# Second products of a two-level seven-product scheme: sums carried in PSUM by ScalarE, parts in another order

## The chip, the cores and the metric

The kernel runs on one core of a Trainium2 chip. The metric is device time in microseconds (us). The profile is of one execution; the engines are named as in it: PE (matmuls), PEld (PE's weight loads), DVE, ACT (ScalarE), POOL and SP.

## The reference

The reference is an attention layer whose mask keeps only keys in the query's hash bucket, and after it an MLP mixer of two stages. Only the last stage matters here. With `x` the attention's output, in the layout (4, 768, 512):

```python
xt = x.transpose(0, 2, 1)
h = np.maximum(xt @ w_tok1, 0.0) @ w_tok2
u = x + h.transpose(0, 2, 1)
h2 = np.maximum(u @ w_ch1, 0.0) @ w_ch2
return (u + h2).astype(np.float32)
```

All of it is in fp32; `w_ch1` is 512 x 1536 and `w_ch2` 1536 x 512. The change lies in the multiplication by `w_ch2`, called the second products below.

## The kernel before

The program has three stretches: attention (to about 310 us of the profile), the token mixer (to about 387 us) and the channel mixer (function `channels`, the rest). The channel mixer works in three steps, s = 0, 1, 2, each on 1024 of the 3072 positions (two halves of 512). A step first computes the hidden rows, R = relu(w_ch1' u), and then the second products (`outputs(s)`).

Both multiplications use Winograd's form of the seven-product scheme, twice over. On the outer level the second product of a step is made of seven products p1 to p7, in the order p1, p5, p7, p6, p3, p2, p4 (`ORDER`). p1 is multiplied out plainly (`whole_product`). Each of the other six goes through `product`, which applies the seven-product scheme again: the left factor (weights) and the right factor are cut into quarters, and seven sums of left quarters are multiplied with seven sums of right quarters. With a00 to a11 the left and b00 to b11 the right quarters, and S1 = a10 + a11, S2 = S1 - a00, S4 = a01 - S2, T1 = b01 - b00, T2 = b11 - T1:

| part | left (its number in `LEFTS`) | right |
|---|---|---|
| m1 | a00 (4) | b00 |
| m2 | a01 (5) | b10 |
| m5 | S1 (0) | T1, in the place of b01 |
| m7 | a00 - a10 (1) | b11 - b01, in `extra()` |
| m6 | S2 (2) | T2 |
| m3 | S4 (3) | b11 |
| m4 | a11 (6) | b10 - T2, in the place of b10 |

With U = m1 + m6 the four blocks of the output are: block 0 = m1 + m2, block 1 = U + m5 + m3, block 2 = U + m7 + m4, block 3 = U + m7 + m5. `qs[:, 0]` to `qs[:, 3]` are these blocks, 128 x 256 each.

A part is three matmuls of 128 x 128 by 128 x 256 (a quarter is three chunks of 128 deep), and an fp32 matmul appears in the profile as two instructions. So a product has 42 matmul instructions. All matmuls are issued by `accumulate` (L780) and all of these ACT copies by `copy` (L786).

PSUM is handed out in pairs of banks, b0 to b3, in a ring: `blocks(2)` takes two pairs, one product uses two and the next the other two. `ps[0]`, `ps[1]` are the two banks of the first pair, `ps[2]`, `ps[3]` of the second.

The order of the work is written by hand (a manual schedule): each engine executes its instructions in the order of the program, and semaphores are derived from what each instruction reads and writes. In a product of before:

1. PE: m1 into ps[0], m2 into ps[1]. ACT copies m1 out (p1). DVE makes T2 in the place of b00 (L1330).
2. PE: m5 into ps[2], m7 into ps[3]. DVE makes b10 - T2 (L1334). ACT copies both m5 and m7 out in one instruction of 128 x 512 (p57).
3. PE: m6 added on ps[0], which makes U; m3 added on ps[2]; m4 added on ps[3]. ACT copies U out.
4. DVE: the work of the list `between` (sums of the outer level, L1292 and L1377, and others), then `begin` for the next product (L1287: `extra()`, L1288: T1), then four additions that finish the blocks (L1352, L1355, L1368, L1369).

`begin(name)` thus prepares the next product's right factor while this one runs. `combine` (L1292) makes the outer level's right sums, four operations of 128 x 768: for p5 it remakes r0, for p7 it remakes r1. `fetch_left` has SP fetch the left factors of the product after the next in two pieces, [0] for the first four of `LEFTS` and [1] for the last three.

`look()` is a side task on ACT: it checks the sizes of q and k to see whether the fast attention was safe. A look is a Square (L1462), a Relu that accumulates, and a read of the accumulator (L1470), all on 128 x 768, followed by a POOL issue that fetches the next piece. It does something on ACT only when three pieces have been fetched ahead. Looks stand after the copy of p1's result (L1395; s + 1 of them, none in the last step) and in each product (one in step 0, two in step 1, none in step 2). `copies()` hands out scratch tiles of 128 x 1024 from three buffers.

In the last step the products p2 and p4 are `final`: their sums are added to the output's values in place and stored from SBUF, p2 by SP, p4's last two blocks by ACT. In p4 of the other steps `inputs` (L606 to L610) prepares the next step's right factors.

Of the kernel before, what the change touches and what calls it, by code (L numbers as in the profile page):

```python
# [48 lines left out]
def kernel(  # L49
# [14 lines left out]
    P = 128  # L64
# [687 lines left out]
    def channels(pool, psum, SW1, second, TA, judge):  # L752
# [32 lines left out]
        def copy(ps, c):  # L785
            nc.scalar.copy(c, ps)  # L786
            return c
# [378 lines left out]

        ORDER = ["p1", "p5", "p7", "p6", "p3", "p2", "p4"]
        WHOLE = ["p1"]
        LEFTS = [4, 5, 0, 1, 2, 3, 6]
        halves = [slice(0, QC), slice(QC, HC)]  # L1170
        passed = second["passed"]

        def prepare():
# [12 lines left out]

                return job

            def parts(w, store, other=False):
                def job():  # L1190
                    (a00, a01), (a10, a11) = weight_quarters(w)
                    n = 4 * QC * P
                    if other:
                        place = area(1)[:, 7 * QC * P : 7 * QC * P + n].rearrange("p (i n) -> p i n", i=4)
                    else:
                        place = pool.tile([P, 2, S], F32, name="seen", tag="seen", bufs=1)
                        place = place.rearrange("p i s -> p (i s)")[:, :n].rearrange("p (i n) -> p i n", i=4)
                    new = [place[:, i].rearrange("p (k c) -> p k c", k=a00.shape[1]) for i in range(4)]
                    nc.vector.tensor_tensor(new[1], a00, a10, op=ALU.subtract)
                    nc.vector.tensor_tensor(new[0], a10, a11, op=ALU.add)  # L1200
                    nc.vector.tensor_tensor(new[2], new[0], a00, op=ALU.subtract)
                    nc.vector.tensor_tensor(new[3], a01, new[2], op=ALU.subtract)
                    store(place, [a00, a01, a11], a10)

                return job

            def second_parts(name):
                def store(place, raw, rest):
                    to = passed[name].rearrange("p (i n) -> p i n", i=7)
                    nc.sync.dma_start(out=to[:, 2:6], in_=place)  # L1210
                    for i, a in zip((0, 1, 6), raw):
                        nc.sync.dma_start(out=to[:, i].rearrange("p (k c) -> p k c", k=QC), in_=a)

                return parts(left[name], store, name == "p2")

            def hidden_parts(name):
                def store(place, raw, rest):
# [52 lines left out]
                    nc.sync.dma_start(out=left_at(g)[:, sl], in_=passed[name][:, sl])  # L1270


        operand = {f"r{i}": [[R[i][:, n, ks] for n in range(2)] for ks in halves] for i in range(4)}
        operand["x"] = [
            [t.rearrange("p a k n -> p (a k n)")[:, n * QC * TT // 2 : (n + 1) * QC * TT // 2].rearrange(
# [8 lines left out]
        def begin(name):  # L1284

            b00, b01, b10, b11 = quarters(name)
            nc.vector.tensor_tensor(extra(), b11, b01, op=ALU.subtract)  # L1287
            nc.vector.tensor_tensor(b01, b01, b00, op=ALU.subtract)  # L1288

        def combine(to, a, op, b, where=[(0, 0), (0, 1), (1, 0), (1, 1)]):  # L1290
            for h, n in where:
# [16 lines left out]
            fetch_left(7 * s + 2)  # L1308
            return pair

        def product(s, j, name, q, between, final=None):

            half = slice(0, TT // 2)
            pairs = blocks(2)
            ps = [a[:, i, half] for a in pairs for i in range(2)]
            w = left_at(7 * s + j).rearrange("p (i k c) -> p i k c", i=7, k=QC)
            b00, b01, b10, b11 = quarters(name)  # L1320
            ks = range(QC)

            def part(i, left, right, start=True):
                accumulate(ps[i], lambda k: w[:, LEFTS.index(left), k], lambda k: right[:, k], ks, start)

            part(0, 4, b00)
            part(1, 5, b10)
            c = copies()
            p1 = copy(ps[0], c[:, half])
            nc.vector.tensor_tensor(b00, b11, b01, op=ALU.subtract)  # L1330
            part(2, 0, b01)
            part(3, 1, extra())
            fetch_left(7 * s + j + 2, [0])
            nc.vector.tensor_tensor(b10, b10, b00, op=ALU.subtract)  # L1334
            p57 = copy(pairs[1][:, :, half], c[:, TT // 2 : TT * 3 // 2].rearrange("p (i t) -> p i t", i=2))
            part(0, 2, b00, False)
            part(2, 3, b11, False)
            u = copy(ps[0], c[:, TT * 3 // 2 :])
            for _ in range(min(s + 1, 2) if s < last else 0):
                look()  # L1340
            part(3, 6, b10, False)
            fetch_left(7 * s + j + 2, [1])
            for work in between:
                work()
            qs = q.rearrange("p i (n t) -> p (i n) t", n=2)

            issuer = nc.scalar if j == 6 else nc.sync
            if j < 6 and not final:
                begin(ORDER[j + 1])
            if final:  # L1350
                nc.vector.tensor_tensor(p1, p1, qs[:, 0], op=ALU.add)
            nc.vector.tensor_tensor(qs[:, 0], ps[1], p1, op=ALU.add)  # L1352
            if final:
                nc.sync.dma_start(out=final(0, 0), in_=qs[:, 0])
            nc.vector.tensor_tensor(p57[:, 0], p57[:, 0], p57[:, 1], op=ALU.add)  # L1355
            if j < 6 and final:
                begin(ORDER[j + 1])
            if final:
                nc.vector.tensor_tensor(qs[:, 3], qs[:, 3], u, op=ALU.add)
                nc.vector.tensor_tensor(qs[:, 3], qs[:, 3], p57[:, 0], op=ALU.add)  # L1360
                nc.sync.dma_start(out=final(1, 1), in_=qs[:, 3])
                for i in (1, 2):
                    nc.vector.tensor_tensor(qs[:, i], qs[:, i], u, op=ALU.add)
                for i, a in [(1, ps[2]), (2, ps[3])]:
                    nc.vector.tensor_tensor(qs[:, i], a, qs[:, i], op=ALU.add)  # L1365
                    issuer.dma_start(out=final(i // 2, i % 2), in_=qs[:, i])
                return
            nc.vector.tensor_tensor(qs[:, 3], p57[:, 0], u, op=ALU.add)  # L1368
            nc.vector.tensor_tensor(  # L1369
                qs[:, 1:3], pairs[1][:, :, half], u[:, None, :].to_broadcast([P, 2, TT // 2]), op=ALU.add,  # L1370
            )

        def outputs(s):
            sl = [slice(TT * (2 * s + i), TT * (2 * s + i) + TT) for i in range(2)]
# [21 lines left out]
            for _ in range(s + 1 if s < last else 0):  # L1396
                look()
            q7, q57, q6, q5 = [output_at(i) for i in range(4)]
            product(s, 1, "p5", q5, [lambda: combine("r0", "x", ALU.subtract, "r0")])
            rest = decide() if judge and s == last else None  # L1400
            product(s, 2, "p7", q7, [lambda: combine("r1", "r2", ALU.subtract, "x")])
            if rest:
                rest()
            product(s, 3, "p6", q6, [add(q57, q7, q5)])
            if rest:
                flags.append(nc.values_load(unsafe, min_val=0, max_val=1))
                tc.mark_branch_hint_location("careful", hint="LikelyTaken", engines=mybir.ALL_ENGINES)
# [2 lines left out]
            def add_residual():  # L1410
                nc.gpsimd.dma_start(out=q7, in_=XT[:, KC:, sl[0]], accum_op=ALU.add)

            product(s, 4, "p3", q3, [
                add(q6, q6, q1), add(q57, q57, q6), store(q57, 1, 1), add(q5, q5, q6), add(q7, q7, q6),
                *([] if s < last else [add_residual]),
            ])
            end = [add(q3, q3, q5), store(q3, 0, 1)]
            if s < last:
                product(s, 5, "p2", q2, [
                    *end, right_sums("p2", s + 1)[0],  # L1420
                    *([lambda h=h: fetch_hidden_left(h) for h in range(5)] if s == 0 else []),
                ])
                product(s, 6, "p4", q4, [
                    add(q2, q2, q1), store(q2, 0, 0), lambda: inputs(s + 1, T, 0), lambda: inputs(s + 1, T, 1),
                ])
                add(q4, q4, q7)()
                store(q4, 1, 0)()
            else:
                def final(at):
                    start = sl[0].start  # L1430
                    return lambda i, n: out[at + i, :, start + TT // 2 * n : start + TT // 2 * (n + 1)]

                product(s, 5, "p2", q1, [
                    *end, add(q1, q1, XT[:, :KC, sl[0]]),
                ], final(0))
                product(s, 6, "p4", q7, [], final(KC))

        def residual(s):

# [43 lines left out]
        def decide():  # L1483

            assert not (unseen or seen)
            top = pool.tile([P, 1], F32, name="top", tag="top", bufs=1)
            nc.vector.tensor_reduce(top, excess, AX.X, ALU.max)
            nc.vector.tensor_scalar(top, top, 1e30, None, op0=ALU.min)

            def rest():  # L1490
                ps = blocks(1)[0][:, 0]
                nc.tensor.transpose(ps[:1, :P], top, ident)  # L1492
                one = pool.tile([1, 1], F32, name="one", tag="one", bufs=1)
                nc.vector.tensor_reduce(one, ps[:1, :P], AX.X, ALU.max)
                nc.vector.tensor_scalar(unsafe, one, 0.0, None, op0=ALU.is_gt)

            return rest
# [150 lines left out]
```

## Time and profile before

| | |
|---|---|
| median of 3 runs | 792.02 us (791.40 to 792.57) |
| profiled execution | 792.34 us |
| its span | 790.5 us |
| PE busy | 782.9 us, 4721 matmul instructions |
| DVE busy | 674.3 us |
| ACT busy | 446.5 us |
| granted clock of PE | 0.999 |

The page of a profile gives busy times by engine, the chain of work that ended last, and groups of instructions. The timeline lists instructions in order of time: start, duration, engine, line, operation, output<-inputs, shapes, count, and in square brackets the idle time of the engine before it with what ended it. A matmul's duration (0.38 us here) overlaps with its successor's; the distance from start to start is 0.216 us for 256 columns.

### The profile page before, as it was taken

To read this page: it belongs to the slowest core of one execution; us is meant where nothing else is said; L and a number is where in the kernel's file an instruction comes from. 1 tells how busy PE (TensorE), PEld (TensorE's weight loads), DVE (VectorE), ACT (ScalarE), POOL (GpSimd) and SP (SyncE) were. 2 spreads that over 40 slices of the span, in tenths; PEclk is the share of its full clock that TensorE was granted. 3 is DMA by queue.
4 is the path that set the end of the run, shared out by engine and by line. 5 is a ranking of instruction groups with operands and counts; after the bars stand their busy time and mean duration, and the time that the engine had idled before them with its cause. 6 is when DMAs were issued, how large, how long until landed. Compare 5 with 4: busy or idle time off the path is not lost.

```text
span 790.5 us, 12412 instructions
## 1 busy us (share of the span) xinstructions
PE 782.9 (99%) x4721; PEld 475.6 (60%) x4721; DVE 674.3 (85%) x925; ACT 446.5 (56%) x730; POOL 53.5 (7%) x77
## 2 busy tenths in 40 slices
PE   8999999999999999999999999999999999999997
PEld 4444444444444444455544458877777887786886
DVE  5989898988887677999697879899779899978986
ACT  6688888888888887333323121326765456674111
POOL 1000000000000000011121010111001122000001
PEclk9999999999999999999999999999999999999999
DMA  4435353537352424795686995799846789820655
GB/s 164 163 123 163 123 164 123 163 123 243 137 180 89 143 66 160 203 273 123 117 268 220 344 379 174 216 305 238 259 134 210 251 230 221 266 84 0 198 167 120
DMA packets 102160, 144.85 MB, mean 183 GB/s; under 512 B 30216, under 2 KB 71888, under 8 KB 102096
## 3 DMA queue, kind: packets, MB, share of 16 engines
q1 hardware_dynamic: 93936, 119.02, 45.8%
q0 software_dynamic: 7728, 24.64, 13.8%
q8 instruction: 38, 0.62, 0.3%
q10 hardware_dynamic: 432, 0.34, 0.1%
q14 instruction: 26, 0.21, 0.1%
HBM read 101.01 MB, written 35.52 MB: 173 GB/s over the span
## 4 chain that ended last, share of the span: by engine, by line
PE 98%; DMA 1%; SPq 0%; DVE 0%; issue 0%
PE b L780 50%; PE sc L353 20%; PE acc L407 16%; PE t L653 5%; PE t L693 5%; PE sums L431 2%; PE hp L301 1%; DMA qk<-in_qk 1%; PE hw L325 0%; SPq L271 0%; DVE second L1365 0%; PE b L1492 0%; SPq L1643 0%
## 5 line engine op out<-in xcount | busy, mean ns | idle before, releaser
L360 ACT ACTIVATE e<-sc 128x768 f32<-128x768 f32 x192 | 154.2, 811 | 11.2 <-PE sc L353 10.8
L353 PE MATMUL sc<-qk 64*128 64x384 f32 x768 | 152.6, 483 | 0.0
L780 PE MATMUL b<-R,second 128*128 128x256 f32 (+1 forms) x612 | 150.9, 404 | 0.0
L780 PEld LDWEIGHTS b<-R,second 128*128 128x128 f32 x612 | 116.2, 190 | 31.7 <-issue 17.2
L407 PE MATMUL acc<-e,vn 128*32 128x384 f32 x1536 | 127.0, 486 | 0.0
L786 ACT COPY c<-b 128x512 f32<-128x512 f32 (+1 forms) x78 | 37.4, 487 | 155.0 <-PE b L780 141.2
L392 DVE TENSOR_TENSOR esd<-esd,e 128x768 f32<-128x768 f32 x96 | 92.0, 958 | 10.4 <-ACT e L360 0.5
L407 PEld LDWEIGHTS acc<-e,vn 128*32 128x32 f32 x1536 | 49.9, 110 | 73.9 <-issue 73.3
L353 PEld LDWEIGHTS sc<-qk 64*128 64x128 f32 x768 | 68.2, 187 | 41.1 <-issue 35.8
L780 PE MATMUL b<-XT,WC 128*128 128x256 f32 (+1 forms) x228 | 73.9, 469 | 0.0
L353 PE MATMUL sc<-bits 64*128 64x384 bf16 x384 | 62.5, 323 | 0.0
L780 PEld LDWEIGHTS b<-XT,WC 128*128 128x128 f32 x228 | 43.3, 190 | 25.3 <-issue 20.8
L388 DVE SCALAR_TENSOR_TENSOR esd<-e 128x768 f32<-128x768 f32 x32 | 30.6, 955 | 23.4 <-ACT e L360 23.3
L780 PE MATMUL b<-XT,SW 128*128 128x256 f32 (+1 forms) x156 | 43.7, 412 | 0.0
L653 PE MATMUL t<-x,W 128*128 128x512 f32 x96 | 41.8, 593 | 0.0
L353 PEld LDWEIGHTS <-bits 64*128 64x128 bf16 x384 | 18.5, 94 | 33.2 <-issue 10.0
L713 POOL DMA_DIRECT2D XT<-second x8 | 9.8, 1228 | 383.5 <-DVE second L712 361.2
L780 PEld LDWEIGHTS b<-XT,SW 128*128 128x128 f32 x156 | 29.6, 190 | 10.0 <-issue 5.1
L452 ACT COPY rec<-rec 32x384 f32<-32x384 f32 x64 | 32.7, 510 | 5.0 <-DVE rec L446 4.2
L413 ACT ACTIVATE num<-acc,vsum 128x384 f32<-128x384 f32 x32 | 18.6, 580 | 29.7 <-PE acc L407 29.3
L780 PE MATMUL b<-TA,WC 128*128 128x256 f32 (+1 forms) x92 | 33.6, 475 | 0.0
L395 DVE TENSOR_TENSOR esd<-esd,e 128x768 f32<-128x768 f32 x32 | 30.5, 954 | 1.9
(245 smaller groups left out, 1172.9 us busy)
## 6 DMA issues: line engine op xcount, KB each, us to landing
second<-left SPq DMA_DIRECT2D x20, 768.0 KB
raw<-in_moe_w_ch SPq DMA_DIRECT2D x16, 768.0 KB
qk<-in_qk SPq DMA_DIRECT2D x15, 768.0 KB
second<-left SPq DMA_DIRECT2D x18, 576.0 KB
seen<-in_qk POOLq DMA_DIRECT2D x21, 384.0 KB, 4.8
WC<-hidden_left SPq DMA_DIRECT2D x18, 448.0 KB
vn<-in_v SPq DMA_DIRECT2D x16, 384.0 KB
vt<-in_vT SPq DMA_DIRECT2D x16, 384.0 KB
```

The lines of the kernel that those rows point to most:

```text
L353: nc.tensor.matmul(sc[:, i, :HALF], t[rows, 1, P * c : P * c + P], t[rows, 0, qs], start=start, stop=not start,)
L360: nc.scalar.activation(e, sc[:, :, :HALF], ACT.Exp, scale=SCALE)
L388: nc.vector.scalar_tensor_tensor(self.d, es[0], NR * EPS, es[1], op0=ALU.add, op1=ALU.add,)
L392: nc.vector.tensor_tensor(self.d, self.d, e, op=ALU.add)
L395: nc.vector.tensor_tensor(self.d, self.d, self.es[-1], op=ALU.add)
L407: nc.tensor.matmul(acc[D * i + d : D * i + d + 32], vn[:, i, c, d : d + 32], e[:, i], start=(c == 0), stop=(c == NR - 1),)
L413: nc.scalar.activation(nums[self.n][:, self.half], acc, ACT.Identity, scale=-1.0, bias=vsum,)
L452: nc.scalar.copy(rec[other : other + 32, h], rec[at : at + 32, h])
L653: nc.tensor.matmul(ps, W1[:, r, P * j : P * j + P], x[:, r], start=(r == 0), stop=(r == NR - 1),)
L693: nc.tensor.matmul(ps[at], left, right, start=start, stop=True, skip_group_check=True,)
L780: nc.tensor.matmul(ps, left(k), right(k), start=start and k == ks[0], stop=stop and k == ks[-1], skip_group_check=True,)
L786: nc.scalar.copy(c, ps)
```

## The change

Two things change in `product`. First, ACT writes into PSUM: m1, once copied out, is written into b0, where m2 is added on it; U is copied from a0 to a1, where m5 and then m3 are added on it. m7 is copied out to c7 before m4 is added on it, and U + m5 to c5 before m3 is. Four additions on DVE become two (block 3 = c7 + c5, block 2 = b1 + u), and ACT copies block 0 and block 1 to their places. Second, the parts come in the order m1, m7, m6, m2, m5, m4, m3. T2 is now made in `begin` in a tile of its own (t2), and what was `between` is now `early`, ahead of b10 - T2 on DVE, or `late`, after the last part. The looks of a product are split into halves between the copies. The left factors are stored in the order in which they are used. In the final products U, c7 and c5 are added from the side, one addition follows the last part, and the stores stand at the end.

```diff
-        LEFTS = [4, 5, 0, 1, 2, 3, 6]
+        LEFTS = [4, 5, 1, 2, 0, 3, 6]
...
             nc.vector.tensor_tensor(b01, b01, b00, op=ALU.subtract)
+            t2 = copies()[:, : QC * TT // 2].rearrange("p (k n) -> p k n", k=QC)
+            nc.vector.tensor_tensor(t2, b11, b01, op=ALU.subtract)
+            begun.append(t2)
...
-        def product(s, j, name, q, between, final=None):
+        def product(s, j, name, q, early, late, final=None):
...
-            part(0, 4, b00)
-            part(1, 5, b10)
-            c = copies()
-            p1 = copy(ps[0], c[:, half])
-            nc.vector.tensor_tensor(b00, b11, b01, op=ALU.subtract)
-            part(2, 0, b01)
-            part(3, 1, extra())
+            t2 = begun.pop()
+            c1, c7, u, c5 = (a[:, i] for a in [split4(copies())] for i in range(4))
...
+            part(a0, 4, b00, True)
+            copy(a0, c1)
+            if looks > 1:
+                begin_look()
+            part(b1, 1, extra(), True)
+            copy(c1, b0)
+            copy(b1, c7)
+            if looks > 1:
+                end_look()
+            part(a0, 2, t2)
+            for work in early:
+                work()
+            if final:
+                plus(qs[:, 3], qs[:, 3], c7)
+            part(b0, 5, b10)
             fetch_left(7 * s + j + 2, [0])
-            nc.vector.tensor_tensor(b10, b10, b00, op=ALU.subtract)
-            p57 = copy(pairs[1][:, :, half], c[:, TT // 2 : TT * 3 // 2].rearrange("p (i t) -> p i t", i=2))
-            part(0, 2, b00, False)
-            part(2, 3, b11, False)
-            u = copy(ps[0], c[:, TT * 3 // 2 :])
-            for _ in range(min(s + 1, 2) if s < last else 0):
-                look()
-            part(3, 6, b10, False)
+            copy(a0, a1)
+            copy(a0, u)
+            nc.vector.tensor_tensor(b10, b10, t2, op=ALU.subtract)
+            part(a1, 0, b01)
+            if final:
+                plus(qs[:, 0], b0, qs[:, 0])
+            else:
+                copy(b0, qs[:, 0])
+            if looks:
+                begin_look()
+            part(b1, 6, b10)
+            copy(a1, c5)
+            if looks:
+                end_look()
+            part(a1, 3, b11)
             fetch_left(7 * s + j + 2, [1])
-            for work in between:
+            for work in late:
                 work()
...
-            if j < 6 and not final:
+            if j < 6:
                 begin(ORDER[j + 1])
...
-            nc.vector.tensor_tensor(qs[:, 0], ps[1], p1, op=ALU.add)
...
-            nc.vector.tensor_tensor(p57[:, 0], p57[:, 0], p57[:, 1], op=ALU.add)
...
-                for i, a in [(1, ps[2]), (2, ps[3])]:
-                    nc.vector.tensor_tensor(qs[:, i], a, qs[:, i], op=ALU.add)
-                    issuer.dma_start(out=final(i // 2, i % 2), in_=qs[:, i])
+            if not final:
+                plus(qs[:, 3], c7, c5)
+                plus(qs[:, 2], b1, u)
+                copy(a1, qs[:, 1])
                 return
-            nc.vector.tensor_tensor(qs[:, 3], p57[:, 0], u, op=ALU.add)
-            nc.vector.tensor_tensor(
-                qs[:, 1:3], pairs[1][:, :, half], u[:, None, :].to_broadcast([P, 2, TT // 2]), op=ALU.add,
-            )
+            plus(qs[:, 2], qs[:, 2], u)
+            plus(qs[:, 3], qs[:, 3], c5)
+            plus(qs[:, 2], b1, qs[:, 2])
+            plus(qs[:, 1], a1, qs[:, 1])
...
+            for i, issuer in zip((0, 3, 2, 1), (nc.sync, nc.sync, nc.scalar, nc.sync)):
+                issuer.dma_start(out=final(i // 2, i % 2, 1), in_=qs[:, i])
...
-            product(s, 1, "p5", q5, [lambda: combine("r0", "x", ALU.subtract, "r0")])
+            product(s, 1, "p5", q5, [lambda: combine("r0", "x", ALU.subtract, "r0")], [])
...
-                add(q6, q6, q1), add(q57, q57, q6), store(q57, 1, 1), add(q5, q5, q6), add(q7, q7, q6),
+                add(q6, q6, q1), add(q5, q5, q6), add(q57, q57, q6), store(q57, 1, 1), add(q7, q7, q6),
...
-                    add(q2, q2, q1), store(q2, 0, 0), lambda: inputs(s + 1, T, 0), lambda: inputs(s + 1, T, 1),
+                    add(q2, q2, q1), store(q2, 0, 0),
+                ], [
+                    lambda: inputs(s + 1, T, 0), lambda: inputs(s + 1, T, 1),
                 ])
```

`plus(to, a, b)` is one DVE addition (L990, a helper that the hidden rows use too). `begin_look` is the Square of a look, `end_look` the rest of it and the fetch of the next piece.

More of the change, by code (lines that the diff above doesn't have):

```diff
@@ L1187, in whole, with parts @@
                 return job
-            def parts(w, store, other=False):
+            def parts(w, store, other=False, order=(0, 1, 2, 3)):
                 def job():
@@ L1197, in job @@
                         place = place.rearrange("p i s -> p (i s)")[:, :n].rearrange("p (i n) -> p i n", i=4)
-                    new = [place[:, i].rearrange("p (k c) -> p k c", k=a00.shape[1]) for i in range(4)]
+                    new = [place[:, order.index(i)].rearrange("p (k c) -> p k c", k=a00.shape[1]) for i in range(4)]
                     nc.vector.tensor_tensor(new[1], a00, a10, op=ALU.subtract)
@@ L1212, in store @@
                         nc.sync.dma_start(out=to[:, i].rearrange("p (k c) -> p k c", k=QC), in_=a)
-                return parts(left[name], store, name == "p2")
+                return parts(left[name], store, name == "p2", LEFTS[2:6])
             def hidden_parts(name):
@@ L1270, in fetch_left @@
                     nc.sync.dma_start(out=left_at(g)[:, sl], in_=passed[name][:, sl])
+        begun = []
         operand = {f"r{i}": [[R[i][:, n, ks] for n in range(2)] for ks in halves] for i in range(4)}
@@ L1309, in whole_product @@
             return pair
-        def product(s, j, name, q, between, final=None):
+        def product(s, j, name, q, early, late, final=None):
             half = slice(0, TT // 2)
-            pairs = blocks(2)
-            ps = [a[:, i, half] for a in pairs for i in range(2)]
+            A, B = blocks(2)
+            a0, a1, b0, b1 = (pair[:, i, half] for pair in (A, B) for i in range(2))
             w = left_at(7 * s + j).rearrange("p (i k c) -> p i k c", i=7, k=QC)
             b00, b01, b10, b11 = quarters(name)
-            ks = range(QC)
-            def part(i, left, right, start=True):
-                accumulate(ps[i], lambda k: w[:, LEFTS.index(left), k], lambda k: right[:, k], ks, start)
-            part(0, 4, b00)
-            part(1, 5, b10)
-            c = copies()
-            p1 = copy(ps[0], c[:, half])
-            nc.vector.tensor_tensor(b00, b11, b01, op=ALU.subtract)
-            part(2, 0, b01)
-            part(3, 1, extra())
-            fetch_left(7 * s + j + 2, [0])
-            nc.vector.tensor_tensor(b10, b10, b00, op=ALU.subtract)
-            p57 = copy(pairs[1][:, :, half], c[:, TT // 2 : TT * 3 // 2].rearrange("p (i t) -> p i t", i=2))
-            part(0, 2, b00, False)
-            part(2, 3, b11, False)
-            u = copy(ps[0], c[:, TT * 3 // 2 :])
-            for _ in range(min(s + 1, 2) if s < last else 0):
-                look()
-            part(3, 6, b10, False)
@@ new lines, in product, with part @@
+            t2 = begun.pop()
+            c1, c7, u, c5 = (a[:, i] for a in [split4(copies())] for i in range(4))
+            qs = q.rearrange("p i (n t) -> p (i n) t", n=2)
+            looks = min(s + 1, 2) if s < last else 0
+            def part(ps, left, right, start=False):
+                accumulate(ps, lambda k: w[:, LEFTS.index(left), k], lambda k: right[:, k], range(QC), start)
+            part(a0, 4, b00, True)
+            copy(a0, c1)
+            if looks > 1:
+                begin_look()
@@ L1342, in product @@
+            if final:
[9 more added lines that the diff above has]
+            part(a1, 3, b11)
             fetch_left(7 * s + j + 2, [1])
-            for work in between:
+            for work in late:
                 work()
-            qs = q.rearrange("p i (n t) -> p (i n) t", n=2)
@@ L1347, in product @@
-            issuer = nc.scalar if j == 6 else nc.sync
-            if j < 6 and not final:
+            if j < 6:
                 begin(ORDER[j + 1])
-            if final:
-                nc.vector.tensor_tensor(p1, p1, qs[:, 0], op=ALU.add)
-            nc.vector.tensor_tensor(qs[:, 0], ps[1], p1, op=ALU.add)
-            if final:
-                nc.sync.dma_start(out=final(0, 0), in_=qs[:, 0])
-            nc.vector.tensor_tensor(p57[:, 0], p57[:, 0], p57[:, 1], op=ALU.add)
-            if j < 6 and final:
-                begin(ORDER[j + 1])
@@ L1358, in product @@
[L1358 to L1363, printed above, removed]
-                for i, a in [(1, ps[2]), (2, ps[3])]:
-                    nc.vector.tensor_tensor(qs[:, i], a, qs[:, i], op=ALU.add)
-                    issuer.dma_start(out=final(i // 2, i % 2), in_=qs[:, i])
-                return
@@ L1373, in outputs @@
+            plus(qs[:, 1], a1, qs[:, 1])
+            if j < 6:
+                nc.sync.dma_start(out=final(0), in_=q[:, 0])
+                for i in range(2):
+                    nc.sync.dma_start(out=final(1, i, 1), in_=qs[:, 2 + i])
+                return
+            for i, issuer in zip((0, 3, 2, 1), (nc.sync, nc.sync, nc.scalar, nc.sync)):
+                issuer.dma_start(out=final(i // 2, i % 2, 1), in_=qs[:, i])
         def outputs(s):
@@ L1398, in outputs @@
             q7, q57, q6, q5 = [output_at(i) for i in range(4)]
-            product(s, 1, "p5", q5, [lambda: combine("r0", "x", ALU.subtract, "r0")])
+            product(s, 1, "p5", q5, [lambda: combine("r0", "x", ALU.subtract, "r0")], [])
             rest = decide() if judge and s == last else None
-            product(s, 2, "p7", q7, [lambda: combine("r1", "r2", ALU.subtract, "x")])
+            product(s, 2, "p7", q7, [lambda: combine("r1", "r2", ALU.subtract, "x")], [])
             if rest:
                 rest()
-            product(s, 3, "p6", q6, [add(q57, q7, q5)])
+            product(s, 3, "p6", q6, [add(q57, q7, q5)], [])
             if rest:
@@ L1413, in outputs @@
             product(s, 4, "p3", q3, [
-                add(q6, q6, q1), add(q57, q57, q6), store(q57, 1, 1), add(q5, q5, q6), add(q7, q7, q6),
+                add(q6, q6, q1), add(q5, q5, q6), add(q57, q57, q6), store(q57, 1, 1), add(q7, q7, q6),
                 *([] if s < last else [add_residual]),
-            ])
+            ], [])
             end = [add(q3, q3, q5), store(q3, 0, 1)]
@@ L1423, in outputs @@
                 product(s, 6, "p4", q4, [
-                    add(q2, q2, q1), store(q2, 0, 0), lambda: inputs(s + 1, T, 0), lambda: inputs(s + 1, T, 1),
+                    add(q2, q2, q1), store(q2, 0, 0),
+                ], [
+                    lambda: inputs(s + 1, T, 0), lambda: inputs(s + 1, T, 1),
                 ])
@@ L1430, in final, with block @@
                     start = sl[0].start
-                    return lambda i, n: out[at + i, :, start + TT // 2 * n : start + TT // 2 * (n + 1)]
+                    def block(i, n=0, count=2):
+                        return out[at + i, :, start + TT // 2 * n : start + TT // 2 * (n + count)]
+                    return block
                 product(s, 5, "p2", q1, [
                     *end, add(q1, q1, XT[:, :KC, sl[0]]),
-                ], final(0))
-                product(s, 6, "p4", q7, [], final(KC))
+                ], [], final(0))
+                product(s, 6, "p4", q7, [], [], final(KC))
         def residual(s):
@@ L1490, in rest @@
             def rest():
-                ps = blocks(1)[0][:, 0]
+                ps = blocks(1)[0][:, 1]
                 nc.tensor.transpose(ps[:1, :P], top, ident)
```

## The prediction

> **What bounds the kernel now.** I read the page's busy shares first, then the chain that ended last, the waits of PE, and then the second products instruction by instruction in the timeline.
>
> ```profile
> PE 782.9 (99%) x4721; PEld 475.6 (60%) x4721; DVE 674.3 (85%) x925; ACT 446.5 (56%) x730; POOL 53.5 (7%) x77
> ```
>
> ```profile
> 387.54 361.04 PE b L780 x1368
> 748.58 0.11 PE b L1492
> 748.69 36.28 PE b L780 x168
> 784.97 0.02 issue
> 784.99 0.17 DVE second L1365
> ```
>
> In the chain, L780 (the helper that issues the matmuls) runs from 387.54 to 784.97 with one transpose in it. The waits of PE list two, 1.1 and 1.0 us, both in the first 8 us. So the matmuls are the bound, nothing near the second products holds them, and the change keeps all of them: 7 parts of 3 fp32 matmuls, each two instructions. Apart from the tail no gain is on offer; the question is whether the new order makes PE wait.
>
> PE's clock in a product: a part starts 1.295 us after the one before (the extra() part of p7 of step 2 starts at 743.24, the next at 744.53), so a product takes 9.07. I count from its first matmul; part n starts at 1.295(n-1). A reader starts 0.20 after the next part's first matmul:
>
> ```profile
> 471.27 0.96 DVE L1330 TENSOR_TENSOR R<-R 128x768 f32<-128x768 f32 x1 [1.83 <-PE b L780]
> ...
> 472.57 0.96 DVE L1334 TENSOR_TENSOR R<-R 128x768 f32<-128x768 f32 x1 [0.34 <-PE b L780]
> ```
>
> These are b00' and b10' of p5 in step 0, which starts at 469.78: 1.49 and 2.79 later, so parts 1 and 2 plus 0.20 each. The other direction is seen in step 1's p5, which starts at 600.01. Here are ACT's and PE's timelines:
>
> ```profile
> 600.21 1.01 ACT L1395 COPY q<-b 128x1024 f32<-128x1024 f32 x1 [6.36 <-PE b L780]
> 601.12 0.85 ACT L1462 ACTIVATE seen<-seen 128x768 f32<-128x768 f32 x1
> 602.00 0.94 ACT L1470 ACTIVATE seen<-seen,minus_safe 128x768 f32<-128x768 f32 x1
> 602.84 0.19 ACT L1470 ACTIVATION_READ_ACCUMULATOR seen<-seen,minus_safe 128x1 f32 x1
> 602.93 0.83 ACT L1462 ACTIVATE looked<-looked 128x768 f32<-128x768 f32 x1
> 603.79 0.94 ACT L1470 ACTIVATE looked<-looked,minus_safe 128x768 f32<-128x768 f32 x1
> 604.63 0.19 ACT L1470 ACTIVATION_READ_ACCUMULATOR looked<-looked,minus_safe 128x1 f32 x1
> 604.72 0.35 ACT L786 COPY c<-b 128x256 f32<-128x256 f32 x1
> 605.12 0.51 PEld L780 LDWEIGHTS b<-R,second 128*128 128x128 f32 x3 [0.18 <-ACT c L786]
> 605.19 0.64 PE L780 MATMUL b<-R,second 128*128 128x256 f32 x2
> ```
>
> The copy of m1 (L786) ends at 605.07 and the weight load that waits for it starts at 605.12: a wait is taken at the weight load, 0.05 after the producer. Unhindered that load runs 0.21 ahead of its matmul. Here it is 0.15 late, and the second matmul comes at 605.447 where the pitch of 0.216 puts it at 605.403: 0.04 lost. So about 0.11 of lateness is forgiven. At 560.91 a load comes 0.33 late and 0.22 is lost, again 0.11 forgiven; there the wait went through a separate semaphore instruction, and producer end (DVE L990, 560.79) to load took 0.12.
>
> **Two places in the Trainium skill.** "PSUM — Partial Sum Buffer", section "Engine vs sequencer instructions", says that ScalarE's queue is strictly first in, first out. The rows above agree: m1 was readable at 601.50, but its copy stood behind q1's copy and two looks until 604.72. The forecast rests on it. "TensorE: Matmul & The Clock Gate", "Step-by-step: what each phase is for", says that weight loads are pulled ahead of running matmuls; here that is worth 0.21 of lead, and the 0.11 measured above is what I use as cushion.
>
> **How far a wait reaches.** In p7 of step 2 (from 739.35) ACT copies only part 1's bank, yet starts at 742.14, which is part 2's end plus 0.20:
>
> ```profile
> 742.14 0.37 ACT L786 COPY c<-b 128x256 f32<-128x256 f32 x1 [4.81 <-PE b L780]
> ```
>
> Part 2 wrote the other bank of the same pair. So I take waits on PSUM to be held for the whole pair, and those on SBUF per region (b00' waited for part 1 alone). This choice is the main fork.
>
> **The change part by part.** Durations: copy of 256 0.37 (L786), Square 0.85, Relu with its accumulator read 1.03 from start to start of the next, a DVE row of 768 0.96.
>
> *(a) Fewer DVE additions.* L1352, L1355, L1368 and L1369 (0.42+0.42+0.42+0.69) become two of 256 wide (0.84); about 1 us less in each of 16 products. Four big operations stay four (t2 replaces b00'). PE hides DVE already, so 0. ACT goes from three copies to eight of 256, about 3.0 us of 9.07: also hidden, apart from the order below.
>
> *(b) m1's copy before part 3, where ACT is late.* Now part 3 adds to a0 and must wait for c1; before, part 5 was the first to do so. In step 1's p5 the two looks after q1's copy stay where they are. c1 ends at 605.07, load at 605.12; its unhindered time is 600.01+2.59-0.21=602.38. Late 2.74, less 0.11: **2.63**. Behind c1 stand the first half look (to 605.84), c1 to b0 (to 606.12) and b1 to c7 (to 606.53): part 4 loads at 606.58 against 606.31, 0.16 lost. Then Relu and read (to 607.46), a0 to a1 (to 607.74), u (to 608.15): part 5 loads at 608.20 against 607.77, 0.32 lost. Together **3.1**. Steps 0 and 2 have no due look there (469.98 and 730.49 show q1's copy alone): 0.
>
> *(c) The other five products of step 1.* c1 1.50–1.87, Square, c1 to b0 from 2.79 (pair wait), c7 to 3.57, Relu and read to 4.51, a1 4.41–4.79, u to 5.20. Part 5's load is due at 4.96 and comes at 5.25: 0.18 each, **0.9**. In steps 0 and 2, without Relu, u ends at 4.87: 0.
>
> *(d) b10' one part ahead of its use.* Before, b10' waited for part 2 and was used by part 7. Now it waits for part 4 and part 6 uses it. It starts at 5.18+0.20=5.38, ends at 6.34, and the load comes at 6.46 through a second semaphore (6.39 without), due at 6.26: 0.09 (0.03). Six products of step 0 and four of step 2: **0.9**. In (c) the later part 5 swallows it.
>
> *(e) The two final products.* The addition on b0 stands behind b10' on DVE and ends at about 6.67. With pair waits part 6 writes the same pair and waits for it: load 6.79, 0.42 each, **0.84**.
>
> *(f) Work moved ahead of b10' on DVE (early).* After b10' come begin (extra, b01, t2, dependent steps of 0.99) and two additions, to about 9.85, 0.8 into the next product. In p5 and p7 four combines at 0.87 end at about 4.5–5.0, in time. p3 has four additions, 4.75 from the trace (500.64 to 505.39), ending at 5.4: 0 to 0.2 each, **0.15** in all. p4's inputs (4.67) now follow b10', leaving DVE about 0.3 later at the next step's start; its addition at 529.60 has 0.3 of idle time in front. 0. The three fetches of left factors on SP still follow parts 4 and 7, after the same reads; POOL's store of q57 moves behind one addition and is not waited for.
>
> *(g) The tail.* L1365 adds twice after the last part (784.99 to 785.74), and ACT issues the second store at 785.90 after its first. Now one addition ends at about 785.41 and SP issues at 785.46: **-0.45**. The final stores of p2 lie 9 us ahead of the end.
>
> Sum: 3.1+0.9+0.9+0.84+0.15-0.45 = **+5.4**. The profiled execution took 792.34 (span 790.5 and 1.8 around it), so 797.8; it was 0.3 above the median of 792.02. I say **797.5**.
>
> **Rivals.**
> - *Waits per bank* (0.20). Then u, c7 and the addition on b0 hold nobody: (b) 2.7, (c) 0, (d) 0.03 x 17 = 0.5, (e) 0, tail -0.45: +2.8, **795.0**. Against it: the copy at 742.14.
> - *DVE late before b10'* (0.16). Its queue ends 0.8 into each product; if semaphores stretch it by 0.4 in p3, p5 and p7 of each step, nine times 0.4 adds 3.6: **801**. The combines' end at 5.0 in step 2's p5 leaves only 0.4. A pause that lowers PE's clock (1.00 everywhere before) would land in the same place.
> - *Not slower* (0.12): the relief of DVE was on the path. Records of PE are modelled, and a hidden wait for DVE in every product would come back. 16 us less on DVE; from a third of it on, it pays the 5.4: **791.5**. Against it: part after part at 1.295 with no exception in the products but the 0.04 at 605.
> - Forecast (0.52).
>
> **How the numbers follow.** Of "not slower" I put 0.04 at faster and 0.08 at same (0.2%, 1.6 us, is about what measurement can tell); all others are slower: 0.88. The likeliest case alone spans 796 to 799.5 ((b) 2.7 to 3.5, (d) 0 to 0.15 each). The range takes in the per-bank case below and half of the DVE case above: 794.3 to 800.8.
>
> **What would show it.** A wait of PE on ACT's c of some 2.7 us at step 1's p5, before its third part; short waits of PE on ACT at part 5 in step 1; weight loads at part 6 waiting for DVE's b10', about 0.09 each and 0.4 in the last p2 and p4; DVE less busy by some 16 us, ACT more by some 30; a single addition after the last matmul. Wrong if the m1 copy of step 1's p5 starts before 604, if parts keep 1.295 throughout, or if PE waits in products of step 0 by more than 0.3.

## The result and the profile after

The changed kernel takes 797.74 us (median of 6 runs, 797.42 to 798.47) against 792.30 (6 runs) for the kernel before: ratio 1.0069, 95% interval 1.0059 to 1.0080, so 4.7 to 6.3 us slower. The forecast was 797.5 us.

The page of the changed kernel:

```profile
span 795.8 us, 12509 instructions
PE 787.4 (99%) x4721; PEld 475.1 (60%) x4721; DVE 656.8 (83%) x887; ACT 472.2 (59%) x816; POOL 53.3 (7%) x77
```

The same 4721 matmul instructions occupy PE 4.5 us longer. DVE is relieved of 17.5 us and ACT carries 25.7 more, near the 16 and 30 of the forecast, and neither number is seen in the time. The chain that ended last of the changed kernel, in order of time (start, duration, what), now leaves PE in four places of its second half. Pieces of less than 0.1 us and those marked `issue` are left out here:

```profile
599.84 1.01 ACT q L1410
600.85 0.75 ACT seen L1483
...
601.62 1.03 ACT seen L1491 x2
602.65 0.74 ACT looked L1483
...
604.26 0.19 ACT looked L1491
604.45 0.27 ACT c L786
...
604.76 148.94 PE b L780 x618
...
777.43 0.96 DVE R L1353
778.39 0.35 DVE q L990
...
778.78 8.05 PE b L780 x36
...
787.73 0.43 DVE second L990
...
788.20 2.87 PE b L780 x12
...
791.10 0.42 DVE second L990
```

The first detour is q1's copy (L1410), two looks (L1483, L1491) and m1's copy (L786) in step 1's p5. The next two are b10 - T2 (L1353, in the second of them only 0.04 us of it and left out above) and the addition on b0 (L990) in the final products. The last line is the single addition after the last matmul.

Smaller losses do not show in the chain. The lengths of the products, from first matmul to first matmul in the trace, show them (us; 9.07 is a product without a wait):

| | p5 | p7 | p6 | p3 | p2 | p4 |
|---|---|---|---|---|---|---|
| before, step 0 | 9.06 | 9.06 | 9.06 | 9.06 | 9.06 | 9.06 |
| before, step 1 | 9.11 | 9.07 | 9.06 | 9.07 | 9.06 | 9.07 |
| before, step 2 | 9.06 | 9.17 | 9.06 | 9.07 | 9.06 | 9.07 |
| after, step 0 | 9.15 | 9.15 | 9.15 | 9.25 | 9.15 | 9.15 |
| after, step 1 | 13.40 | 9.27 | 9.27 | 9.27 | 9.27 | 9.27 |
| after, step 2 | 9.15 | 9.26 | 9.15 | 9.26 | 9.43 | 9.42 |

(Step 2's p7 holds a transpose of the safety check, 0.11 in both kernels.) The products lose 7.1 us in all, 4.3 of them in one. In that one PE does not only wait. Here are three windows of the changed kernel (stretch, length, busy time and count for PE, PEld, DVE, ACT and POOL, granted PE clock, DMA share, GB/s):

```profile
600.00:604.60 4.60, 2.39 (x12) 1.75 (x10) 4.59 (x6) 4.53 (x8) 0.54 (x1) 1.00 0.83 291
604.65:608.05 3.40, 3.29 (x8) 2.67 (x9) 0.00 (x0) 2.69 (x7) 1.08 (x2) 0.50 0.78 244
608.50:611.00 2.50, 2.50 (x13) 2.05 (x12) 1.74 (x2) 1.56 (x4) 0.00 (x0) 1.00 0.80 197
```

After the pause the clock is 0.50, and there the matmuls stand 0.427 us apart instead of 0.216. The pause cost 2.53 us (2.748 between two matmuls, less 0.216), the first matmul at the low clock 0.37, and the other seven 1.34; the last of them reaches only in part into the stretch. Part 6 lost 0.085, as it does in steps 0 and 2. Parts 4 and 5 did not wait.

The trace's record of the clock reads 1.00 from 3.89 to 604.64, 0.50 to 608.05 and 1.00 to 795.79. So the low stretch lasts 3.41 us, and the other two are 176 and 55 times as long. Not every execution has such a stretch: the six that were timed have a mean clock of 0.998, 0.997 and 0.998 (797.69 us, which is the profiled one, 798.47 and 797.90) and of 1.000 (797.56, 797.78 and 797.42). As 3.41 us at 0.50 would by themselves bring the mean to 0.998, the last three had none.

### The profile page after: what moved, and what is told of

The parts are those of the page before. It is cut to its first block, busy times and chain, and to the rows that moved or that the text cites. A ratio compares the mean times of both kernels' runs of the same rounds, so it can differ in the third digit from the quotient of the medians.

```text
span 795.8 us, 12509 instructions
## 1 busy us (share of the span) xinstructions
PE 787.4 (99%) x4721; PEld 475.1 (60%) x4721; DVE 656.8 (83%) x887; ACT 472.2 (59%) x816; POOL 53.3 (7%) x77
## 4 chain that ended last, share of the span: by engine, by line
PE 98%; ACT 1%; DVE 0%; issue 0%; DVEq 0%
PE b L780 50%; PE sc L353 20%; PE acc L407 16%; PE t L653 5%; PE t L693 5%; PE sums L431 2%; PE hp L301 1%; PE idle L470 0%; PE hw L325 0%; ACT seen L1491 0%; ACT q L1410 0%; DVE R L1353 0%; DVE second L990 0%; ACT seen L1483 0%; ACT looked L1483 0%
## 5 line engine op out<-in xcount | busy, mean ns | idle before, releaser
L780 PE MATMUL b<-R,second 128*128 128x256 f32 (+1 forms) x522 | 134.1, 412 | 0.2
L780 PEld LDWEIGHTS b<-R,second 128*128 128x128 f32 x522 | 98.3, 190 | 33.3 <-issue 19.4
L392 DVE TENSOR_TENSOR esd<-esd,e 128x768 f32<-128x768 f32 x96 | 92.0, 958 | 10.4 <-ACT e L360 0.5
L786 ACT COPY c<-b 128x256 f32<-128x256 f32 (+1 forms) x96 | 40.2, 426 | 82.5 <-PE b L780 72.6
L780 PE MATMUL b<-XT,WC 128*128 128x256 f32 (+1 forms) x228 | 73.9, 469 | 0.0
L780 PEld LDWEIGHTS b<-XT,WC 128*128 128x128 f32 x228 | 43.3, 190 | 25.3 <-issue 20.8
L780 PE MATMUL b<-XT,SW 128*128 128x256 f32 (+1 forms) x156 | 43.7, 412 | 0.0
L780 PEld LDWEIGHTS b<-XT,SW 128*128 128x128 f32 x156 | 29.6, 190 | 10.0 <-issue 5.1
L780 PE MATMUL b<-TA,WC 128*128 128x256 f32 (+1 forms) x92 | 33.6, 475 | 0.0
L1353 DVE TENSOR_TENSOR R<-R,c 128x768 f32<-128x768 f32 x15 | 14.4, 957 | 22.6 <-PE b L780 22.6
```

The lines of the kernel that those rows point to most:

```text
L392: nc.vector.tensor_tensor(self.d, self.d, e, op=ALU.add)
L780: nc.tensor.matmul(ps, left(k), right(k), start=start and k == ks[0], stop=stop and k == ks[-1], skip_group_check=True,)
```

## The experiments

The first four ran on one chip with the kernel before beside them (792.18, 30 runs).

**Looks ahead of q1's copy.**

```diff
-            nc.scalar.copy(q1, ps)
             for _ in range(s + 1 if s < last else 0):
                 look()
+            nc.scalar.copy(q1, ps)
```

> The changed kernel with one edit: the looks that stand after the copy of p1's result stand ahead of it, so ACT does them while p1 is multiplied. In the changed kernel the product p5 of step 1 lasts 13.4 us instead of 9.07. Theory A (m1's copy stands behind the two looks, and the pause it makes also lowers PE's clock for some matmuls): p5 of step 1 falls to about 9.3 as its neighbours in that step, 4.1 us less, about 793.6 against 797.7. Rival B (only the pause as the prediction summed it, 3.1): about 2.9 less, 794.8. Rival C (the looks have no part in it; the pause comes from PSUM writes of ACT as such): no gain, 797.7.

Measured: 794.31 (9 runs), ratio 1.0026 (1.0016 to 1.0036); p5 of step 1 lasts 9.27. PE's list of waits:

```profile
PE idle L470 <- DVE ones L97: 1.1, 1, 1.1
```

Nothing of L780 is left in it. The time alone lies between A and B; the product's length decides for A: 4.12 us less than 13.40. What is left above 9.07, 0.20, is that of its neighbours. The looks were the cause of the pause, and the low clock went with it. The medians differ by 3.4 us only, which fits the three executions of the changed kernel that had no low clock. Rival C falls.

**Only one of the two looks ahead.**

```diff
+            if s == 1:
+                look()
             nc.scalar.copy(q1, ps)
-            for _ in range(s + 1 if s < last else 0):
+            for _ in range(1 if s < last else 0):
                 look()
```

> As the looks-first kernel, but in step 1 only one of the two looks is ahead of the copy of p1's result and one stays behind it. The pause before part 3 of p5 is then about 2.6 - 1.85 = 0.8 us. Theory A1 (the clock falls only after a pause of some length, and 0.8 us is under it): p5 of step 1 lasts about 9.07 + 0.8 + 0.2 = 10.1 us at a granted clock of 1.00. Rival A2 (any pause that shows lowers the clock): about 11.4 us with some matmuls at 0.43 us from start to start. In time: 0.8 or 2.1 us above the looks-first kernel.

Measured: 795.08 (6 runs), 1.0038 (1.0025 to 1.0051); p5 lasts 10.34. The pause was 0.74, 0.10 went at the matmul after it, two more waits (parts 4 and 5) took 0.13 and 0.31, and no matmuls stood at 0.427. The mean clock is 1.000 in all six executions: it stayed, A1.

**b10 - T2 in another place.**

```diff
-            nc.vector.tensor_tensor(b10, b10, t2, op=ALU.subtract)
+            nc.vector.tensor_tensor(b00, b10, t2, op=ALU.subtract)
...
-            part(b1, 6, b10)
+            part(b1, 6, b00)
```

> The looks-first kernel with one more edit: b10 - T2 is written into the place of b00, free since part 1, and not over b10, so it has no need to wait for part 4 to end; part 6 reads it there. Theory A (the wait for part 4 and DVE's 0.96 us are what makes part 6 late): the 0.085 us lost in nine products and the 0.36 us in each of the two final ones vanish, about 1.3 us less than the looks-first kernel, 792.3; p3 keeps a part, since DVE is late there on its own account, and step 1 keeps its 0.2 per product, which comes from ACT. Rival D (part 6 waits for ACT's copy of block 0, or for the added semaphore alone): no gain, 793.6.

Measured: 792.60 (12 runs), 1.0002 (0.9993 to 1.0010). All products of steps 0 and 2 are back at 9.06 to 9.07 (p7 of step 2 at 9.17, as before); those of step 1 stay at 9.27. DVE's timeline in step 0's p5, which begins at 470.0:

```profile
472.34 1.82 DVE L1296 TENSOR_TENSOR R<-TB,R 128x768 f32<-128x768 f32 x2
474.08 0.95 DVE L1353 TENSOR_TENSOR R<-R,c 128x768 f32<-128x768 f32 x1
474.95 0.95 DVE L1288 TENSOR_TENSOR second<-R 128x768 f32<-128x768 f32 x1
```

L1353 follows the combines without a gap and no longer waits for part 4. The loss at part 6 was this wait, and D falls. p3's extra loss went too, which I had expected to stay: with b10 - T2 early in every product DVE reaches p3 earlier (its first addition starts 0.61 us into step 0's p3, against 0.82 in the looks-first kernel).

**Two of DVE's additions left out of the kernel before.**

```diff
-            nc.vector.tensor_tensor(p57[:, 0], p57[:, 0], p57[:, 1], op=ALU.add)
+            if final:
+                nc.vector.tensor_tensor(p57[:, 0], p57[:, 0], p57[:, 1], op=ALU.add)
...
-            nc.vector.tensor_tensor(qs[:, 3], p57[:, 0], u, op=ALU.add)
...
+            nc.scalar.copy(qs[:, 3], p57[:, 0])
```

> The kernel before, with two of DVE's additions left out of each of the 16 products that are not final: m5 + m7 and the addition of U for block 3; ACT copies m5 alone to block 3's place. So block 3 lacks m7 and U. DVE has about 0.8 us less in each product, 13 us in all, about what the change relieves it of. Theory A (PE never waited for DVE in these products): 792.3 as before, within 0.2%. Rival E (the relief of DVE was on the path): 1 to 5 us faster.

Measured: 792.31 (12 runs), 1.0002 (0.9993 to 1.0011), with DVE busy 663.2 us against 674.3:

```profile
PE 783.5 (99%) x4721; PEld 475.8 (60%) x4721; DVE 663.2 (84%) x893; ACT 451.6 (57%) x746; POOL 53.6 (7%) x77
```

11 us less on DVE bring nothing. The products are those of the kernel before, to 0.01. Rival E, and with it "not slower", falls.

The next three, and the kernel with three looks further down, have 792.12 (15 runs) for the kernel before beside them.

**Step 1's first look of a product moved behind the second.** The two halves that stand under `looks > 1` are removed, and a whole look follows the late one:

```diff
             if looks:
                 end_look()
+            if looks > 1:
+                look()
             part(a1, 3, b11)
```

> The looks-first kernel with one more edit: in step 1 the first look of a product no longer stands in halves between the early copies, but whole behind the second one, after the copy to c5. Theory A (in step 1 part 5 waits for the copy to u, which the Relu of that look delays): the 0.2 us lost in each of its six products falls to the 0.085 that steps 0 and 2 lose at part 6; 0.7 us less than the looks-first kernel. Rival F (ACT's PSUM writes cost the 0.2, the look has no part): no gain.

Measured: 793.84 (10 runs), 1.0022 (1.0013 to 1.0032). Five of step 1's products fall to 9.15, p3 rises to 9.34. So what step 1 lost beyond the other steps came from the look ahead of the copies; F falls. The products gain 0.53 us of the 0.7.

**The copy to u behind part 5.**

```diff
             copy(a0, a1)
-            copy(a0, u)
             nc.vector.tensor_tensor(b10, b10, t2, op=ALU.subtract)
             part(a1, 0, b01)
+            copy(a0, u)
```

> The looks-first kernel with the copy of U to u moved behind part 5 in the program (part 5 writes a1, u is read from a0, the other bank of the same pair). Theory A (waits on PSUM are held for the whole pair): the copy starts only at part 5's end, 6.7 us into the product; in steps 0 and 1 the Square behind it delays the copy to c5, and part 7 comes about 1.1 us late in each of 12 products: 12 to 13 us slower than the looks-first kernel. Rival B (waits are held per bank): the copy starts at 4.5 to 4.8 as before, and nothing gets slower.

Measured in one run: 808.49; the products are 13.8 us longer than in the looks-first kernel. ACT's timeline in step 0's p7, which starts at 480.0:

```profile
484.09 0.36 ACT L786 COPY b<-b 128x256 f32<-128x256 f32 x1 [0.46 <-PE b L780]
486.68 0.37 ACT L786 COPY c<-b 128x256 f32<-128x256 f32 x1 [2.23 <-PE b L780]
486.95 0.38 ACT L786 COPY second<-b 128x256 f32<-128x256 f32 x1
```

The first line is a0 to a1, the second u. It reads the bank that the first has just read, and yet waits 2.23 us until part 5 has written the other bank: waits on PSUM do cover the pair. My sum had the place wrong, though. I had part 7 late in the 12 products with a due look. Instead part 6 is late by 1.0 in all 16 products that are not final: it writes b1 and waits for the copy of block 0 out of b0 (486.95), the same rule on the other pair. PE's list of waits has them in one line (total, times, longest; it counts from the modelled end of the matmul before, so 1.0 shows as about 0.7):

```profile
PE b L780 <- ACT second L786: 11.8, 16, 0.8
```

**Everything moved.** The looks-first kernel with step 1's looks late and b10 - T2 in the place of b00, directly after `part(a0, 2, t2)`, ahead of `early`; beside the edits already shown:

```diff
             part(a0, 2, t2)
+            nc.vector.tensor_tensor(b00, b10, t2, op=ALU.subtract)
             for work in early:
                 work()
...
-            nc.vector.tensor_tensor(b10, b10, t2, op=ALU.subtract)
             part(a1, 0, b01)
```

> Looks ahead of the copy of p1's result, looks of step 1 late, b10 - T2 in the place of b00 and ahead of the early work on DVE. Theory A: no product waits any more, all last 9.07, and the tail's gain of 0.7 us is left: about 0.7 below the kernel before, 791.5, which is within what the measurement tells. Rival G (writing sums into PSUM costs PE something of its own): products above 9.07.

A miss: 795.27 (5 runs), 1.0040 (1.0026 to 1.0053). All products last 9.06 to 9.07, apart from step 2's p7 (9.17) and p6 (9.26) and the three p3, 10.33 each. Timelines of DVE and ACT in step 0's p3, which starts at 497.46:

```profile
498.95 0.96 DVE L1341 TENSOR_TENSOR R<-R,c 128x768 f32<-128x768 f32 x1 [2.17 <-PE b L780]
499.83 1.22 DVE L1390 TENSOR_TENSOR second<-second,q 128x1024 f32<-128x1024 f32 x1
...
501.93 0.37 ACT L786 COPY c<-b 128x256 f32<-128x256 f32 x1
504.67 0.37 ACT L786 COPY second<-b 128x256 f32<-128x256 f32 x1 [2.36 <-DVE second L1390]
504.94 0.85 ACT L1481 ACTIVATE seen<-seen 128x768 f32<-128x768 f32 x1
```

p3's output takes q6's place, which DVE's four early additions (L1390) still read. b10 - T2 (L1341), put ahead of them, must first wait for part 1, which reads b00, and DVE is idle for 2.17 us. So the additions end 7.1 us into the product, against 5.4 in the kernel of the third experiment. The copy of block 0 waits for them, and part 6 waits for that copy, again over the pair. G falls with the products at 9.06 to 9.07: ACT's writing into PSUM costs PE nothing by itself. Step 2's p6 loses its 0.2 at part 4, behind two late copies of ACT; what held these was not followed.

**b10 - T2 behind the early work again.** The edits of the looks-first, the looks-late and the other-place kernels together; against the kernel with everything moved:

```diff
             part(a0, 2, t2)
-            nc.vector.tensor_tensor(b00, b10, t2, op=ALU.subtract)
...
             copy(a0, u)
+            nc.vector.tensor_tensor(b00, b10, t2, op=ALU.subtract)
             part(a1, 0, b01)
```

> Looks ahead of the copy of p1's result, looks of step 1 late, b10 - T2 in the place of b00 but where the changed kernel has it, behind the early work on DVE. In the kernel with everything moved, p3 alone lost 1.27 us, because b10 - T2 ahead of p3's four additions made them end later, ACT's copy into q6's place waited for them, and the copy to c5 stood behind it. Theory A: with b10 - T2 behind the additions all products last 9.07, except p3 of step 1, where the late look may cost up to 0.2; the tail's 0.7 is left: 791.6, ratio 0.9993 to the kernel before. Rival H (p3's loss came from the other place for b10 - T2): p3 loses about 1.2 again, 795.

Measured beside 792.06 (17 runs) for the kernel before: 791.54 (13 runs), 0.9995 (0.9987 to 1.0003). All products are at 9.06 to 9.07, apart from the transpose in step 2's p7 and from p3 of step 1 (9.42, more than the 0.2 allowed). There the late look delays ACT's copy of the last block of p6, DVE's four additions wait for that copy, and the copy of block 0 waits for the additions:

```profile
627.27 1.23 DVE L1390 TENSOR_TENSOR second<-second,q 128x1024 f32<-128x1024 f32 x1 [1.66 <-ACT second L786]
632.11 0.37 ACT L786 COPY second<-b 128x256 f32<-128x256 f32 x1 [0.99 <-DVE second L1390]
```

This is the change with nearly all of its waits taken out, and it equals the kernel before within what can be told. H falls. The expectation names the copy to c5 for p3's loss in the kernel with everything moved; by the trace it was part 6, which waited for the copy of block 0.

**Three looks.** The changed kernel with one more look in step 1.

```diff
             for _ in range(s + 1 if s < last else 0):
                 look()
+            if s == 1:
+                look()
```

> The changed kernel with a third look behind the copy of p1's result in step 1. The pause before part 3 of p5 grows by one look, 1.85 us, to about 4.4. Theory A1 (the low clock lasts some 2.5 us after a pause, however long it was beyond its threshold): p5 lasts 13.4 + 1.85 = 15.3. Rival A2 (the low clock lasts longer after a longer pause): 16 or more, with more than seven matmuls at 0.43.

Measured in one run: 800.52; p5 lasts 15.17. The windows before, in and after the stretch at the low clock:

```profile
603.40:607.80 4.40, 0.34 (x2) 0.00 (x0) 2.54 (x3) 4.33 (x9) 1.08 (x2) 0.99 1.01 364
607.74:611.13 3.39, 3.23 (x8) 2.60 (x9) 0.00 (x0) 2.79 (x7) 0.54 (x1) 0.50 0.70 208
611.50:614.00 2.50, 2.50 (x13) 2.02 (x13) 1.62 (x2) 1.57 (x5) 0.23 (x1) 1.00 0.66 175
```

The pause grew from 2.53 to 4.33, the stretch at the low clock did not: the record has it from 607.73 to 611.14, again 3.41 us. A1, with 3.41 in place of the 2.5 expected.

**A pause in between.** The one-look-first kernel with q1's copy made twice in step 1.

```diff
             nc.scalar.copy(q1, ps)
+            if s == 1:
+                nc.scalar.copy(q1, ps)
```

> As the kernel with one look first, but in step 1 the copy of p1's result is made twice, 1.0 us more on ACT ahead of m1's copy. The pause before part 3 of p5 is about 1.75 us, between the 0.74 after which the clock stayed and the 2.53 after which it fell. No theory says which; p5 lasts 11.3 us if the clock stays at 1.00, about 12.5 if it falls to a half as after 2.53.

Measured in one run, beside 792.06 for the kernel before: 795.92; the pause is 1.79, p5 lasts 11.39, and the clock stays at 1.00:

```profile
604.90:607.50 2.60, 2.60 (x12) 1.77 (x10) 0.20 (x1) 2.54 (x7) 0.54 (x2) 1.00 0.67 210
```

After the pause 0.54 more is lost, in the matmul behind it and at parts 4 and 5.

**The tail alone.** The kernel before, with p4's last store issued by SP.

```diff
-                    issuer.dma_start(out=final(i // 2, i % 2), in_=qs[:, i])
+                    (nc.sync if i == 2 else issuer).dma_start(out=final(i // 2, i % 2), in_=qs[:, i])
```

> The kernel before with one edit at the end: SP issues the store that follows the very last addition, ACT only the one before it. From the last matmul's start to the end of the span the kernel before takes 5.89 us, the changed one 5.12. Theory T1 (the gain of 0.77 is one addition, 0.33, and the issue that stands behind another on ACT, 0.13, and the rest is where the last store's semaphore stands in the list that SP waits through): 5.75 to 5.2 here, with the addition still in it. Rival T2 (it is all the addition): 5.89.

Measured in one run: 792.46; 5.93 from the last matmul to the end, against 5.89. The store is issued 0.13 earlier, as summed, but lands 0.17 later after its issue. It kept the semaphore that SP waits for first, so T1's last term was not tried. The run does not decide between T1 and T2.

## Why the prediction was right

By its own steps, from the trace, where the pair of profiles lets each be measured:

| step | forecast | measured |
|---|---|---|
| (a) fewer additions | 0 | 0 (left out alone: ratio 1.0002) |
| (b) m1's copy behind the looks, p5 of step 1 | 3.1 | 4.3 |
| (c) other products of step 1 | 0.9 | 1.0 |
| (d) b10 - T2 one part ahead of its use, with p3 | 0.9 | 0.85 |
| (e) the final products | 0.84 | 0.72 |
| (f) DVE late in p3 | 0.15 | 0.2 |
| (g) tail | -0.45 | -0.77 |
| sum | 5.4 | 6.3 |

The bound, the reach of the waits, the sign of each step and, outside (b), the place of each wait held. In (d) p3 of steps 0 and 2 is counted with 0.085 each and their remaining 0.1 each stands in (f).

(b) was mis-sized for the profiled execution. The pause was 2.53 against 2.63 forecast. The clock was the term left out: I had named a drop only as something that would land in the place of a rival, at no price. It cost about 1.6 us (1.34, and 0.37 less the 0.10 that the shorter pauses show too). In return the waits at parts 4 and 5, forecast at 0.16 and 0.32, did not come, and part 6 lost 0.085 in their place. Without the low clock (b) comes to 3.1, as forecast: this is an estimate from 2.53 and from the 0.54 behind the pause of 1.79. The page "TensorE: Matmul & The Clock Gate" of the Trainium skill puts the idle time that lowers the clock at one window of about 3.4 us ("Part 1: The HAM clock gate"); here a pause of 2.53 sufficed and one of 1.79 did not.

(g) gained 0.46 from the missing addition (0.33) and from the issue that no longer stands behind another (0.13), as summed: the last store is issued 0.87 after the last matmul's start, against 1.33. The rest is in SP's waits, as the two traces have them. In the kernel before, SP waits first for the store that lands last (788.22), and then for seven further semaphores some 0.07 to 0.10 apart, which takes 0.54; in the changed kernel that store's semaphore is the eighth, and nothing of this list is left behind it. Its landing took 0.22 longer after the issue. 0.46 and 0.54 less 0.22 is 0.78, against the 0.77 measured. No run moved the semaphore alone, so the 0.54 is read from these two traces and not tried.

The profiles' spans differ by 5.3 and not 6.3, because the changed kernel's profile reached the first matmul of the channel mixer 0.99 earlier (386.38 against 387.38): the second group of its first matmuls waited 0.95 for a piece of q and k in the kernel before and not in the changed one. In the other 11 profiles that start lies between 386.4 and 387.9, whichever kernel it is, so I do not count it to the change.

The medians give 5.4, with 6.3 at the upper edge of the interval. So the closeness of 797.74 to 797.5 is partly luck. For the profiled execution the forecast was about 1 us short of what the trace adds up to. For the three executions without the low clock the same sum, with 3.1 for (b), is 5.1, and the median lies between the two. This is argued and not shown: the times of the two kinds lie only 0.3 apart, where the sums differ by 1.2.

Of the rivals, waits per bank falls by the copy at 486.68. DVE behind by 0.4 in p3, p5 and p7 did not come: those lose 0.085 to 0.2. "Not slower" falls by the additions left out.

## What to carry to other kernels

Where PE is never idle, work taken off another engine is worth nothing (here 11 us of DVE's), and every new hand-over to and from that engine has to be placed against PE's clock: when is the value ready, what stands ahead of it in the engine's queue, when is the weight load due. Side work that was harmless behind a late use becomes the bound when the use moves up: here, two checks in ACT's queue cost 4.1 of the 7.1 us that the products lost in the profile, and moving them ahead of one copy gives that back. Before a dependency is placed close, look at what the buffer's waits cover (here both banks of a pair), and write a result into a dead buffer rather than over an operand still being read.

## What the runs showed that I had not expected

- A pause of PE of 2.53 us, and one of 4.33, lowered its clock to 0.50 for 3.41 us; pauses of 0.74 and 1.79 did not. Each is one profile, and the length need not be what decides. In all 13 traces every stretch of the clock's record that ends within it is a whole number of 3.41 us steps (176, 1 and 55 in the changed kernel, 230 in the kernel before). Counted in these steps, PE was idle for 71% of the one before the low clock in the changed kernel and for all of it with three looks; the two pauses without effect filled 22% and 52% of a step. So it may matter where in a step a pause falls, which would also explain why three of the six timed executions of the changed kernel show no low clock. No run here tries it.
- A late weight load is forgiven about 0.11 us also in the changed kernel: in p7 of step 1 the load starts at 618.31, 0.05 after the copy to u ends, 0.31 behind its time, and 0.20 is lost.
- Moving one DVE operation of 0.96 us ahead of others that are not on PE's path cost 1.27 us in each p3, by way of its own wait for PE and of ACT.
